# Second half's first layer norm computed in the turned layout: x loaded transposed, statistics spread over the partitions, in place of TensorE transposes

## The chip, the cores and the metric

The kernel runs on one core of one Trainium2 chip. The metric is device time in microseconds from the first to the last instruction of one execution. All arithmetic is float32; products are made of float32r operands (an upper and a lower part of each value).

## The reference

```python
y = _layernorm(x)                       # x: (2048, 1024), eps 1e-5
q, k, v = y @ wq, y @ wk, y @ wv        # 32 heads of 32, 4 segments of 512 tokens
# in each segment s: causal softmax attention inside the segment, and a read of the memory (M, z)
o = g * (phi(qs) @ M) / (phi(qs) @ z + 1e-6) + (1 - g) * softmax(qs @ ks.T * scale + mask) @ vs
M, z = M + phi(ks).T @ vs, z + sum(phi(ks))
h = x + o @ wo
out = h + gelu_tanh(_layernorm(_layernorm(h)) @ w1 + b1) @ w2 + b2     # d_ff 3584
```

The two layer norms of the last line stand for the block's own and the one ahead of it; the first line's is the one that the change touches.

## The kernel before

The 2048 tokens are worked off in two halves of 1024, each of two segments of 512. A half goes through four stages: attention, the output projection with the residual, the second layer norm, and the first MLP product (a scheme of fewer, larger block products: first a "lead", then 14 "pairs" of `Mixer.pair`). The second MLP product for all tokens comes at the end, in the second half.

Every product x @ w is made of three matmuls: upper by upper, upper by lower, lower by upper (`mm3`, lines 127 to 129 of the profile). So every activation and weight exists as an upper part (a cast to float32r) and a lower part (value minus upper part). The inputs of the attention, `yh` and `yl`, lie turned: 128 features on the partitions, tokens along the free dimension, 8 chunks of features by 512 tokens for each segment.

`ln1` makes them for one segment of 512 tokens. It loads four row tiles `xt` of 128 tokens by 1024 features. For each, VectorE takes mean and variance (lines 134 and 138), GpSimd makes the scale and the offset (lines 141, 142, 147), ScalarE scales the whole tile (line 182), and `ln_transpose` turns it: eight TensorE transposes in two groups of four (line 161), each group into one PSUM bank of tags "av" and "pt", then ScalarE's copy to `yh` (line 163) and VectorE's subtraction to `yl` (line 165).

The attention of a half is 16 units of 24 steps. A step is one chunk of one projection (three matmuls), and behind it whatever a table of steps (`at`, `close`) puts there: weight loads and splits (`wload`, `wsplit`, lines 688, 695, 699), score matmuls (line 569), their reduction on VectorE (571), exponentials on ScalarE (573), and so on. The steps 0 to 7 of a unit make `kps`, 8 to 15 `qps`, 16 to 23 `vps`. Units 0 and 1 read segment 0; unit 2 is the first that reads segment 1. A weight block is loaded (`wr`, two buffers), its upper part cast on VectorE or ScalarE, and its lower part made by GpSimd in four pieces of two chunks each, 128x256.

Segment 0 of the second half is normalised in the last nine pairs of the first half's MLP; segment 1 is begun there and goes on in units 0 and 1 of the second half's attention. There `interleave` and a counter take one piece of the side work per so many steps of the main work: 0.17 per step (three matmuls) in the pairs, 0.55 per step in the attention. The order of instructions on each engine is the order in which the program emits them (`in_order`), and each engine waits in that order.

In the pairs, each `Mixer.pair` makes five products of 12 matmuls (line 1014) in 20 steps: `dps` in a bank of tag "pt" (two banks), `bps` in tag "d" (three). VectorE adds out of these banks (lines 1038, 1156, 1169), ScalarE applies the activation (1031), GpSimd combines weights (1126 to 1129), ScalarE and VectorE split them (1141, 1142).

Of the kernel before, what the change touches and what calls it, by code (L numbers as in the profile page):

```python
# [4 lines left out]

# [12 lines left out]
P = 128  # L18
S = 2048
D = 1024  # L20
# [27 lines left out]
def raw(ap):  # L48
    return ap.bitcast(F32)


def build(tc, x, wq, wk, wv, wo, beta, w1, b1, w2, b2, out):
    nc = tc.nc
    top = ExitStack()
    const = top.enter_context(tc.tile_pool(name="const", bufs=1))
# [100 lines left out]
    def ln_transpose(src, xh, xl, t4, tags, slow=False):  # L156
        for c in range(2):
            pt = ln_bank(tags).rearrange("p (a b) -> p a b", a=4)
            for i in range(4):
                k = 4 * c + i  # L160
                nc.tensor.transpose(pt[:, i, :], src[:, k * P:(k + 1) * P], ident)
            hi = xh[:, 4 * c:4 * c + 4, t4 * P:(t4 + 1) * P]
            nc.scalar.copy(hi, pt)
            yield
            nc.vector.tensor_tensor(xl[:, 4 * c:4 * c + 4, t4 * P:(t4 + 1) * P], pt, raw(hi),  # L165
                                    op=ALU.subtract)
            if slow:
                yield
# [36 lines left out]
    def chain(*gens):  # L205
        for g in gens:
            yield from g
# [6 lines left out]
    def ln1(half, sl, delay=0, aside=None, gap=1):  # L214
        xs = []
        for t in range(4):
            xt = lnp.tile([P, D], F32, tag="ln", name="xt", bufs=4)
            r0 = half * HT + (4 * sl + t) * P
            nc.sync.dma_start(xt, x[0, r0:r0 + P, :])
            xs.append(xt)  # L220
        for _ in range(delay):
            yield

        def home():
            if ("y", half, sl) not in acts:
                acts["y", half, sl] = acts["y", sl] = seg_tiles(sl, "y")
            return acts["y", sl]

        yield from ln_tiles(lnp, xs, None, None, False, act=True, aside=aside, gap=gap,
                            fold=lambda src, t4: ln_transpose(src, *home(), t4, ("av", "pt", "pt"), slow=True))  # L230

    def opening():

# [1203 lines left out]
    for half in range(2):  # L1437
# [15 lines left out]
        if half == 0:  # L1453
            nc.sync.dma_start(mz_dram, acts["mz"])
        ab.release()
        zx = acts["zx"] = tc.alloc_tile_pool(name=f"zx{half}", bufs=1, side="right", reuse_waits="tile")
        mq = tc.alloc_tile_pool(name=f"mq{half}", bufs=1, side="right", reuse_waits="tile")
        pp = tc.alloc_tile_pool(name=f"post{half}", bufs=1, reuse_waits="tile")
# [93 lines left out]
    top.close()  # L1552


_INS = ["A_x", "A_wq", "A_wk", "A_wv", "A_wo", "A_beta", "B_w1", "B_b1", "B_w2", "B_b2"]


# [16 lines left out]
```

## Time and profile before

| what | value |
|---|---|
| three runs | 2185.11, 2191.39, 2191.93 us; median 2191.39 |
| the profiled execution | 2187.23 us, span 2185.5 us |
| TensorE busy | 2157.7 us, 99% of the span |
| VectorE, ScalarE, GpSimd busy | 1349.0, 1102.1 and 959.7 us |
| moved by DMA | 376.20 MB, mean 172 GB/s |

A busy TensorE is one with a matmul in flight: matmuls overlap, so a duration of 0.39 us belongs to a matmul that starts 0.227 us after the one before it. In rows of the chain, the times are those by which the chain went on. In this profile the engines are PE (TensorE), DVE (VectorE), ACT (ScalarE), POOL (GpSimd) and SP (the queue that issues most DMAs); L161 is line 161 of the kernel. A pointed bracket names what ended the idle time before an instruction.

### The profile page before, as it was taken

The page shows a single profiled execution, that of the slowest core. Times are in us where ns is not written, and L with a number is a line of the kernel's source. Part 1 is how long each engine was busy: PE and PEld are TensorE (multiplying, and loading weights), DVE is VectorE, ACT ScalarE, POOL GpSimd, SP SyncE. Part 2 cuts the span into 40 slices and gives each one's busy share as a digit, 9 for nine tenths or more (in the row PEclk, how much of TensorE's full clock was granted, in tenths as well). Part 3 has the DMA queues.
Part 4 walks back from the last instruction along what each step waited for, and adds up shares of the span by engine and source line. Part 5 has one row for each costly group of instructions (what it writes and reads, how often), then busy time and mean ns, then how long its engine had stood idle before and what let it go on. Part 6 is the DMA issues. An engine that isn't in the chain of part 4 may idle for free.

```text
span 2185.5 us, 33210 instructions
## 1 busy us (share of the span) xinstructions
PE 2157.7 (99%) x10937; PEld 1750.4 (80%) x10937; DVE 1349.0 (62%) x2696; ACT 1102.1 (50%) x2433; POOL 959.7 (44%) x1206
## 2 busy tenths in 40 slices
PE   7999999999999999999999999999999999999999
PEld 6777777778888888877777768888887888888887
DVE  6766666665745556766667655745666665576653
ACT  5777777762543445777777752643443232322221
POOL 5534345562444434533335561534446544256330
PEclk9999999999999999999999999999999999999999
DMA  6544445664465655544444663575569865676762
GB/s 182 134 106 107 105 107 136 190 203 164 154 207 155 187 158 147 136 107 109 106 108 133 198 197 141 173 217 162 171 199 373 274 226 185 190 244 230 250 222 92
DMA packets 352405, 376.20 MB, mean 172 GB/s; under 512 B 27214, under 2 KB 244330, under 8 KB 352234
## 3 DMA queue, kind: packets, MB, share of 16 engines
q1 hardware_dynamic: 288778, 336.98, 50.7%
q10 hardware_dynamic: 63456, 37.10, 5.6%
q8 instruction: 87, 1.43, 0.3%
q14 instruction: 84, 0.69, 0.1%
HBM read 241.27 MB, written 82.38 MB: 148 GB/s over the span
## 4 chain that ended last, share of the span: by engine, by line
PE 91%; DVE 2%; DMA 2%; POOL 2%; ACT 1%; issue 1%; SPq 0%; ACTq 0%; DVEq 0%; POOLq 0%
PE po L1410 22%; PE bps L1014 10%; PE cps L1014 7%; PE dps L1014 7%; PE pst L619 4%; PE po L633 3%; PE pqk L569 3%; PE kps L127 3%; PE vps L127 3%; PE qps L127 3%; PE kps L128 3%; PE pwo L127 2%; PE kps L129 2%; PE vps L128 2%; PE pwo L129 2%; PE pwo L128 2%
## 5 line engine op out<-in xcount | busy, mean ns | idle before, releaser
L571 DVE CUSTOM_DVE_ANT_0 pqk<-pqk,mask 128x512 f32<-128x512 f32 (+2 forms) x384 | 216.9, 565 | 241.6 <-PE pqk L569 214.8
L573 ACT ACTIVATE junk<-pqk,mx 128x512 f32<-128x512 f32 (+2 forms) x384 | 225.2, 587 | 134.7 <-DVE mx L571 128.2
L626 POOL TENSOR_SCALAR_AFFINE_SELECT e<-e 128x128 f32<-128x128 f32 (+1 forms) x384 | 137.6, 359 | 268.9 <-ACT e L622 254.1
L699 POOL TENSOR_TENSOR wl<-wr,wh 128x256 fp32r<-128x256 f32 x268 | 202.1, 770 | 108.7 <-PE pqk L569 85.8
L622 ACT ACTIVATE e<-pst 128x384 f32<-128x384 f32 (+1 forms) x384 | 200.8, 529 | 70.9 <-PE pst L619 69.5
L1420 DVE TENSOR_TENSOR c<-c,po 128x512 f32<-128x512 f32 x160 | 105.4, 684 | 156.7 <-PE po L1410 153.9
L569 PE MATMUL pqk<-ks,qs 96*128 96x512 f32 (+2 forms) x384 | 138.6, 361 | 5.7 <-ACT junk L573 3.0
L619 PE MATMUL pst<-qs,ks 104*128 104x512 f32 (+3 forms) x512 | 140.9, 318 | 1.0 <-ACT e L622 0.4
L619 PEld LDWEIGHTS pst<-qs,ks 104*128 104x128 f32 x512 | 95.7, 188 | 34.7 <-ACT e L622 10.7
L1410 PE MATMUL po<-w2h,zh 128*128 128x512 f32 x378 | 120.9, 389 | 0.4 <-DVE zh L1350 0.4
L1267 POOL TENSOR_TENSOR w2r<-w2r 128x512 f32<-128x512 f32 x54 | 84.6, 1579 | 72.3 <-DMA w2r<-in_B_w 72.3
L127 PE MATMUL kps<-yh,wh 128*128 128x512 f32 (+1 forms) x264 | 113.5, 430 | 0.0
L127 PE MATMUL qps<-yh,wh 128*128 128x512 f32 x256 | 113.2, 442 | 0.0
L1014 PE MATMUL bps<-zh,sb 128*128 128x512 f32 x336 | 110.9, 391 | 0.0
L1014 PE MATMUL bps<-zh,sa 128*128 128x512 f32 x336 | 110.8, 390 | 0.0
L1126 POOL TENSOR_TENSOR s<-r 128x512 f32<-128x512 f32 x28 | 44.3, 1583 | 141.0 <-DVE sa L1142 81.3
L127 PE MATMUL vps<-yh,wh 128*128 128x512 f32 x256 | 105.0, 410 | 0.0
L1410 PE MATMUL po<-w2h,hl 128*128 128x512 f32 x322 | 103.2, 390 | 0.7 <-DVE hl L1350 0.4
L128 PE MATMUL kps<-yl,wh 128*128 128x512 f32 (+1 forms) x264 | 102.8, 389 | 0.5 <-DVE yl L165 0.4
L129 PE MATMUL kps<-yh,wl 128*128 128x512 f32 (+1 forms) x264 | 102.2, 387 | 0.0
L128 PE MATMUL qps<-yl,wh 128*128 128x512 f32 x256 | 101.0, 394 | 0.0
L128 PE MATMUL vps<-yl,wh 128*128 128x512 f32 x256 | 100.8, 394 | 0.0
(271 smaller groups left out, 6204.0 us busy)
## 6 DMA issues: line engine op xcount, KB each, us to landing
hr<-h_dram SPq DMA_DIRECT2D x112, 448.0 KB, 5.5
w2r<-in_B_w SPq DMA_DIRECT2D x122, 256.0 KB, 4.2
r<-in_B_w SPq DMA_DIRECT2D x56, 512.0 KB, 4.6
ks<-kk SPq DMA_DIRECT2D x360, 64.0 KB, 2.0
qs<-qq SPq DMA_DIRECT2D x360, 64.0 KB, 2.0
h_dram<-ht ACTq DMA_DIRECT2D x84, 256.0 KB, 3.6
wx<-in_B_w SPq DMA_DIRECT2D x56, 256.0 KB, 3.5
o_dram<-side SPq DMA_DIRECT2D x52, 256.0 KB, 4.2
```

The costliest lines, as they stand in the source:

```text
L127: nc.tensor.matmul(ps, ah, bh, start=first, stop=False)
L128: nc.tensor.matmul(ps, ah, bl, start=False, stop=False)
L129: acts["mm"] = nc.tensor.matmul(ps, al, bh, start=False, stop=last)
L569: nc.tensor.matmul(ps, u["qs"][0:96, j, i * P:(i + 1) * P], u["ks"][0:96, j, 0:n], start=True, stop=True)
L571: nc.vector.tensor_tensor_reduce(out=ps, in0=ps, in1=mask[:, 512 - n:512], op0=ALU.add, op1=ALU.min, scale=-SCALE, scalar=3.0e38, accum_out=m)
L573: at(now[0] + 1, lambda: nc.scalar.activation(acts["junk"][:, :n], ps, AF.Exp, bias=m, scale=-1.0, accum_out=u["mx"][:, 1, i, j:j + 1]))
L619: nc.tensor.matmul(ps[:, o:o + 512 - P * jk], u["ks"][:, j, jk * P:(jk + 1) * P], u["qs"][:, j, jk * P:512], start=True, stop=True)
L622: nc.scalar.activation(e, ps[:, :w], AF.Exp, scale=SCALE)
L626: nc.gpsimd.affine_select(d, d, pattern=[[0, 2], [1, P]] if n == 2 else [[1, P]], compare_op=ALU.is_ge, fill=0.0, base=0, channel_multipli ...
L699: nc.gpsimd.tensor_tensor(l[:, c], wr[:, c], raw(h)[:, c], op=ALU.subtract)
L1014: nc.tensor.matmul(ps, x_[:, c, :], y_[:, c, :], start=first and c == 0 and n == 0, stop=last and c == 3 and n == 2, skip_group_check=True)
L1410: nc.tensor.matmul(ps, x_[:, k], y_[k], start=opens and k == 0 and i == 0, stop=closes and k == self.KP - 1 and i == 2, skip_group_check=True)
```

## The change

The host passes a second copy of x, transposed (`xt_`). The new class `Columns` normalises a segment without turning its tiles. From the row tiles it takes only the statistics: `rn` holds, for each of 4 tiles, the scale r of 128 tokens and the offset -mean * r (8 columns). One TensorE transpose turns `rn` to 8x128, ScalarE copies it out, a DMA stores it to DRAM, and another loads it back to all partitions as `rows`: 512 scales and 512 offsets. The turned x is loaded in four tiles `xc` of 128 partitions by two chunks by 512 tokens, and for each, `apply` multiplies by the scales and adds the offsets, `upper` copies to `yh`, `lower` subtracts to `yl`.

A table of steps says when each piece is emitted. Both segments' statistics, loads and `rows`, and the four rounds of segment 0, come in the last nine pairs, one step per 1/0.22 steps of the pairs; there VectorE multiplies and adds. The four rounds of segment 1 come in the attention, where VectorE multiplies and GpSimd adds; with 0.55 pieces per step they reach to about step 38.

```diff
+    rn_dram = {k: dram.tile([8, P], F32, name=f"rn_dram{k[0]}{k[1]}") for k in ((1, 0), (1, 1))}
...
+    class Columns:
+        def __init__(self, half, sl):
+            self.half, self.sl, self.plan = half, sl, {}
+            self.rn = acts["rnp"].tile([P, 8], F32, name="rn", bufs=2)
...
+        def load(self, t):
+            self.xs[t] = lnp.tile([P, D], F32, tag="ln", name="xt", bufs=4)
+            r0 = self.half * HT + (4 * self.sl + t) * P
+            nc.sync.dma_start(self.xs[t], x[0, r0:r0 + P, :])
+        def stats(self, t):
...
+            nc.vector.bn_aggr(mv, st)
...
+            nc.gpsimd.tensor_tensor(r, v[:, 0:1], mhalf, op=ALU.pow)
+            nc.gpsimd.tensor_scalar(rn[:, 4 + t:5 + t], mv[:, 0:1], -1.0, r, op0=ALU.mult, op1=ALU.mult)
+        def turn(self):
+            ps = psum.tile([P, 512], F32, tag="av", name="prn", bufs=1)[0:8, 0:P]
+            nc.tensor.transpose(ps, self.rn, ident)
+            self.rt = acts["rnp"].tile([P, P], F32, name="rt", bufs=1)[0:8, :]
+            nc.scalar.copy(self.rt, ps)
+        def keep(self):
+            nc.sync.dma_start(rn_dram[self.half, self.sl], self.rt)
+        def spread(self):
+            self.rows = acts["rnp"].tile([P, 2, 512], F32, name="rows", bufs=1)
+            nc.sync.dma_start(self.rows.rearrange("p a n -> p (a n)"),
+                              rn_dram[self.half, self.sl].rearrange("k p -> (k p)").partition_broadcast(P))
+        def columns(self, c):
+            t0 = self.half * HT + 512 * self.sl
+            self.ws[c] = w = lnp.tile([P, 2, 512], F32, tag="ln", name="xc", bufs=4)
+            nc.sync.dma_start(w, xt_[256 * c:256 * c + 256, t0:t0 + 512].rearrange("(c p) n -> p c n", p=P))
+        def apply(self, c, i, eng):
+            w, row = self.ws[c], self.rows[:, i, :].unsqueeze(1).to_broadcast([P, 2, 512])
+            eng.tensor_tensor(w, w, row, op=ALU.add if i else ALU.mult)
...
+        def upper(self, c):
+            nc.scalar.copy(self.home(0, c), self.ws[c])
+        def lower(self, c):
+            nc.vector.tensor_tensor(self.home(1, c), self.ws[c], raw(self.home(0, c)), op=ALU.subtract)
...
+        def columns_at(self, *steps, lag, add):
+            for c, m in enumerate(steps):
+                self.at(m, partial(self.apply, c, 0, nc.vector))
+                self.at(m + 1, partial(self.apply, c, 1, add))
+                self.at(m + lag, partial(self.upper, c))
+                self.at(m + lag + 1, partial(self.lower, c))
...
-            acts["ahead"] = ln1(1, 1, gap=2)
-            interleave(chain(*(mixer.pair(j) for j in range(HP - 9, HP))),
-                       chain(ln1(1, 0, 2), islice(acts["ahead"], 3)), 0.17)
+            acts["rnp"] = tc.alloc_tile_pool(name="rn1", bufs=1, reuse_waits="tile")
+            one, two = Columns(1, 0), Columns(1, 1)
+            for t in range(4):
+                one.at(0, partial(one.load, t))
+                one.at(6 + t, partial(one.columns, t))
+                two.at(19 + 3 * t, partial(two.load, t))
+                two.at(25 + 3 * t, partial(two.columns, t))
+            one.rows_at(3, 4, 5, 6, turn=9, keep=10, spread=12)
+            one.columns_at(15, 18, 21, 24, lag=2, add=nc.vector)
+            two.rows_at(22, 25, 28, 31, turn=34, keep=35, spread=37)
+            interleave(chain(*(mixer.pair(j) for j in range(HP - 9, HP))), steps(one, two), 0.22)
+            two.columns_at(4, 8, 12, 16, lag=3, add=nc.gpsimd)
+            acts["ahead"] = steps(two)
...
+    inputs = {**inputs, "A_xT": np.asarray(inputs["A_x"])[0].T}
```

Two places in the order of instructions, first as it stands before, then with the change. GpSimd, from the last split of the first weight blocks into unit 1 of the second half's attention (`wl` are the low parts of weight blocks; `v`, `nb` belong to the layer norm, `xc` are the turned columns, `mask` and `pat` constants):

```order
L104 TENSOR_TENSOR wl<-wr,wh 128x1024 x2
L141 TENSOR_SCALAR v<-mv 128x1
L142 TENSOR_TENSOR v<-v,mhalf 128x1
L147 TENSOR_SCALAR nb<-mv,v 128x1
L341 MEMSET mask 128x512
L518 MEMSET pat 8x4
L342 AFFINE_SELECT mask<-mask 128x128
L519 AFFINE_SELECT pat<-pat 8x4
L521 AFFINE_SELECT pat<-pat 8x4
L699 TENSOR_TENSOR wl<-wr,wh 128x256 x4
L141 TENSOR_SCALAR v<-mv 128x1
L142 TENSOR_TENSOR v<-v,mhalf 128x1
```

```order
L104 TENSOR_TENSOR wl<-wr,wh 128x1024 x2
L428 MEMSET mask 128x512
L605 MEMSET pat 8x4
L429 AFFINE_SELECT mask<-mask 128x128
L606 AFFINE_SELECT pat<-pat 8x4
L608 AFFINE_SELECT pat<-pat 8x4
L786 TENSOR_TENSOR wl<-wr,wh 128x256 x4
L281 TENSOR_TENSOR xc<-xc,rows 128x1024 x2
L786 TENSOR_TENSOR wl<-wr,wh 128x256 x5
L281 TENSOR_TENSOR xc<-xc,rows 128x1024
L786 TENSOR_TENSOR wl<-wr,wh 128x256 x4
L281 TENSOR_TENSOR xc<-xc,rows 128x1024
```

Where small pieces of the layer norm stood, four additions of 128x1024 stand: two of them between the value weights of unit 0 (the first four pieces) and the key weights of unit 1 (the first four of the next five). VectorE, from unit 0's first lower part (`side<-kps`) to the first score reduction (`pqk`):

```order
L440 TENSOR_TENSOR side<-kps,side 128x512
L682 CAST ks_8733<-pat 8x2048
L165 TENSOR_TENSOR yl_8801<-pt,yh_8800 128x4x128
L382 SCALAR_TENSOR_TENSOR pk,zc<-e,r 128x512
L165 TENSOR_TENSOR yl_8801<-pt,yh_8800 128x4x128
L682 CAST ks_8734<-pat 8x2048
L134 BN_STATS st<-xt 128x6 x2
L138 BN_AGGR mv<-st 128x2
L440 TENSOR_TENSOR side<-qps,side 128x512
L682 CAST identr<-ident 128x128
L695 CAST wh<-wr 128x1024
```

```order
L527 TENSOR_TENSOR side<-kps,side 128x512
L769 CAST ks_8747<-pat 8x2048
L281 TENSOR_TENSOR xc<-xc,rows 128x1024
L469 SCALAR_TENSOR_TENSOR pk,zc<-e,r 128x512
L769 CAST ks_8748<-pat 8x2048
L527 TENSOR_TENSOR side<-qps,side 128x512
L292 TENSOR_TENSOR yl_8849<-xc,yh_8848 128x1024
L281 TENSOR_TENSOR xc<-xc,rows 128x1024
L769 CAST identr<-ident 128x128
L782 CAST wh<-wr 128x1024
```

The subtractions out of PSUM and the statistics are gone; the first round's subtraction (`yl`) and the second round's multiplication (`xc`) stand ahead of the cast of unit 1's key weights (`wh`). On ScalarE the upper copy of the first round stands ahead of the copy of `qps`, and that of the second behind the two exponentials of `qps`.

## Rows read from the trace of the kernel before

**Rows 1.** The page: busy time by engine, and the chain's shares by engine.

```profile
PE 2157.7 (99%) x10937; PEld 1750.4 (80%) x10937; DVE 1349.0 (62%) x2696; ACT 1102.1 (50%) x2433; POOL 959.7 (44%) x1206
...
PE 91%; DVE 2%; DMA 2%; POOL 2%; ACT 1%; issue 1%; SPq 0%; ACTq 0%; DVEq 0%; POOLq 0%
```

**Rows 2.** Stretches: us, busy time (instructions) of each engine, clock, DMA share, GB/s.

```profile
717.00:836.60 119.60, 118.72 (x539) 97.95 (x538) 69.19 (x105) 50.60 (x77) 46.65 (x45) 1.00 0.53 156
836.60:881.60 45.00, 44.09 (x226) 36.04 (x226) 33.58 (x80) 27.19 (x61) 24.49 (x42) 1.00 0.61 162
881.60:926.60 45.00, 45.00 (x258) 36.63 (x257) 30.90 (x98) 32.20 (x91) 23.33 (x44) 1.00 0.49 129
```

**Rows 3.** Chain of waits in the pairs: start, us on the chain, engine, tile, line.

```profile
740.69 0.44 PE pt L161 x4
...
784.79 5.44 PE bps L1014 x24
...
810.77 0.70 DVE ht L1038
811.61 2.96 PE dps L1014 x12
```

**Rows 4.** The transposes of line 161 on TensorE between 700 and 900 us.

```profile
L161 PE MATMUL pt<-ident,xt x64: 270/272/273, 740.5 to 878.4; 128*128 128x128 f32 x64
```

**Rows 5.** Groups of the whole trace, by shape: busy us, mean ns | idle before.

```profile
L926 DVE TENSOR_TENSOR hb<-ht,b2c 128x1024 f32<-128x1024 f32 x16 | 19.2, 1209 | 0.5 <-DMA h_dram<-hb 0.4
...
L1126 POOL TENSOR_TENSOR s<-r 128x512 f32<-128x512 f32 x28 | 44.3, 1583 | 141.0 <-DVE sa L1142 81.3 <-DVE sb L1142 39.7 <-DMA r<-in_B_w 12.6
...
L104 POOL TENSOR_TENSOR wl<-wr,wh 128x1024 fp32r<-128x1024 f32 x2 | 4.8, 2406 | 6.5 <-issue 6.2 <-ACT wh L103 0.4
...
L695 ACT CAST wh<-wr 128x1024 fp32r<-128x1024 f32 x1 | 1.0, 1032 | 0.0
```

**Rows 6.** Timeline of VectorE in a pair: start, us, instruction.

```profile
701.11 2.99 DVE L1142 TENSOR_TENSOR sb<-s,sb 128x512 fp32r<-128x512 f32 x3 [1.85 <-ACT sb L1141]
...
707.34 0.68 DVE L1142 TENSOR_TENSOR sb<-r,sb 128x512 fp32r<-128x512 f32 x1
```

**Rows 7.** Timeline of GpSimd in the same pair.

```profile
701.93 1.61 POOL L1126 TENSOR_TENSOR s<-r 128x512 f32<-128x512 f32 x1 [5.47 <-DVE sb L1142]
```

**Rows 8.** Timeline of ScalarE in unit 0 of the second half's attention.

```profile
840.37 1.25 ACT L182 ACTIVATE xt<-xt,nb,v 128x1024 f32<-128x1024 f32 x1 [2.00 <-POOL nb L147]
...
843.86 0.59 ACT L434 CAST side<-kps 128x512 fp32r<-128x512 f32 x1
...
848.70 0.59 ACT L434 CAST side<-qps 128x512 fp32r<-128x512 f32 x1 [1.92 <-PE qps L129]
```

**Rows 9.** Timeline of VectorE in units 0 and 1.

```profile
844.48 0.69 DVE L440 TENSOR_TENSOR side<-kps,side 128x512 fp32r<-128x512 f32 x1 [5.44 <-ACT side L434]
845.21 1.40 DVE L682 CAST ks<-pat 8x2048 fp32r<-8x2048 f32 x1
...
852.53 0.69 DVE L695 CAST wh<-wr 128x1024 fp32r<-128x1024 f32 x1 [0.52 <-DMA wr<-in_A_wk]
...
858.08 0.69 DVE L695 CAST wh<-wr 128x1024 fp32r<-128x1024 f32 x1
...
868.19 0.69 DVE L695 CAST wh<-wr 128x1024 fp32r<-128x1024 f32 x1 [0.52 <-DMA wr<-in_A_wk]
```

**Rows 10.** Timeline of GpSimd: low parts of unit 1's key weights, four pieces.

```profile
853.36 3.28 POOL L699 TENSOR_TENSOR wl<-wr,wh 128x256 fp32r<-128x256 f32 x4 [0.74 <-DVE wh L695]
```

**Rows 11.** Timeline of TensorE in unit 1.

```profile
856.01 0.40 PE L129 MATMUL kps<-yh,wl 128*128 128x512 f32 x1
...
867.30 0.50 PE L569 MATMUL pqk<-ks,qs 96*128 96x512 f32 x1
...
870.47 0.44 PE L569 MATMUL pqk<-ks,qs 96*128 96x384 f32 x1 [0.83 <-ACT junk L573]
```

**Rows 12.** Timeline of the SP queue: the load of unit 2's key weights.

```profile
863.93 0.37 SPq L688 DMA_DIRECT2D wr<-in_A_wk  x1
```

More of the change, by code (lines that the diff above doesn't have):

```diff
@@ L3 @@
 from functools import partial
-from itertools import islice
 import concourse.bass as bass
@@ L49, in raw, with build @@
     return ap.bitcast(F32)
-def build(tc, x, wq, wk, wv, wo, beta, w1, b1, w2, b2, out):
+def build(tc, x, xt_, wq, wk, wv, wo, beta, w1, b1, w2, b2, out):
     nc = tc.nc
@@ L230, in ln1, with at, home, rows_at @@
                             fold=lambda src, t4: ln_transpose(src, *home(), t4, ("av", "pt", "pt"), slow=True))
+    class Columns:
+        def __init__(self, half, sl):
+            self.half, self.sl, self.plan = half, sl, {}
+            self.rn = acts["rnp"].tile([P, 8], F32, name="rn", bufs=2)
+            self.xs, self.ws = {}, {}
+        def at(self, step, *fns):
+            self.plan.setdefault(step, []).extend(fns)
+        def load(self, t):
[3 more added lines that the diff above has]
+        def stats(self, t):
+            rn = self.rn
+            st = lnp.tile([P, 2, 6], F32, name="st", bufs=3)
+            for i in range(2):
+                nc.vector.bn_stats(st[:, i, :], self.xs[t][:, 512 * i:512 * i + 512])
+            mv = lnp.tile([P, 2], F32, name="mv", bufs=3)
+            nc.vector.bn_aggr(mv, st)
+            v = lnp.tile([P, 2], F32, name="v", bufs=3)
+            r = rn[:, t:t + 1]
+            nc.gpsimd.tensor_scalar(v[:, 0:1], mv[:, 1:2], 1.0, EPS, op0=ALU.mult, op1=ALU.add)
+            nc.gpsimd.tensor_tensor(r, v[:, 0:1], mhalf, op=ALU.pow)
[18 more added lines that the diff above has]
+            eng.tensor_tensor(w, w, row, op=ALU.add if i else ALU.mult)
+        def home(self, i, c):
+            if ("y", self.half, self.sl) not in acts:
+                acts["y", self.half, self.sl] = acts["y", self.sl] = seg_tiles(self.sl, "y")
+            return acts["y", self.sl][i][:, 2 * c:2 * c + 2, :]
+        def upper(self, c):
+            nc.scalar.copy(self.home(0, c), self.ws[c])
+        def lower(self, c):
+            nc.vector.tensor_tensor(self.home(1, c), self.ws[c], raw(self.home(0, c)), op=ALU.subtract)
+        def rows_at(self, *steps, turn, keep, spread):
+            for t, m in enumerate(steps):
+                self.at(m, partial(self.stats, t))
+            self.at(turn, self.turn)
+            self.at(keep, self.keep)
+            self.at(spread, self.spread)
+        def columns_at(self, *steps, lag, add):
[4 more added lines that the diff above has]
+                self.at(m + lag + 1, partial(self.lower, c))
@@ L232, in opening, with steps @@
+    def steps(*plans):
+        plan = {}
+        for p_ in plans:
+            for m, fns in p_.plan.items():
+                plan.setdefault(m, []).extend(fns)
+            p_.plan = {}
+        for m in range(max(plan) + 1):
+            for f in plan.get(m, ()):
+                f()
+            yield
     def opening():
@@ L1455, in build @@
         ab.release()
+        if "rnp" in acts:
+            acts.pop("rnp").release()
         zx = acts["zx"] = tc.alloc_tile_pool(name=f"zx{half}", bufs=1, side="right", reuse_waits="tile")
@@ L1552, in build @@
     top.close()
-_INS = ["A_x", "A_wq", "A_wk", "A_wv", "A_wo", "A_beta", "B_w1", "B_b1", "B_w2", "B_b2"]
+_INS = ["A_x", "A_xT", "A_wq", "A_wk", "A_wv", "A_wo", "A_beta", "B_w1", "B_b1", "B_w2", "B_b2"]
 def kernel(**inputs):
```

## The prediction

> **What bounds the kernel now.** I read the page's busy times and its chain first. TensorE is busy for 99% of the span and carries 91% of the chain that ends last [rows 1]: an instruction taken off TensorE is worth its own time, and anything that makes TensorE wait costs in full. Then the stretches around the change: the last nine pairs of the first half, the 45 us of the first two attention units of the second half, and the 45 us behind them [rows 2]. TensorE idles about 0.9 us in each of the first two and nothing in the third, so no later idle time absorbs a loss. The chain and the timelines, read next, show which wait ends last.
>
> In the pairs the 24 matmuls of a piece take 5.44 us, 0.227 us each, back to back [rows 3]. Two things interrupt them: groups of four transposes, 0.44 us of chain each, and one wait of 0.84 us (811.61 - 810.77) for VectorE's addition out of `dps`, which holds the "pt" bank that the next `dps` needs; the transposes take banks from the same tag.
>
> In the attention, TensorE waits once, at 870.47, for 0.83 us [rows 11]. The chain behind it: the load of a weight block is issued at 863.93 [rows 12], VectorE casts it at 868.19 [rows 9], and the score reduction queued behind that cast lets TensorE go on. That load starts when GpSimd has finished the low parts of an earlier block (two buffers). So this place is tight on VectorE, ScalarE and GpSimd, though none is the busiest.
>
> **The change, part by part.** *Transposes.* 64 leave TensorE between 740 and 878 us [rows 4], 16 groups, half in the pairs, half in the attention: 8 x 0.44 = 3.5 us in each. Two transposes of the 128x8 statistics come in; they are not in the trace. Bounds: nothing, or a whole group (0.44) each; I take 0.1 each, a quarter of a group.
>
> *Banks.* The layer norm's transposes no longer take "pt" banks in the pairs, so the 0.84 us wait goes, with the pipeline refill behind it about 0.9.
>
> *Pairs, the other engines.* VectorE gets eight 128x1024 multiplications and additions and four subtractions at 1.21 us, the row of the same shape with all operands in SBUF [rows 5], for eight 512-wide subtractions: some 9 us more over about 40 us in which it is busy 58% [rows 2]. Two in a row delay an addition out of PSUM by 2.4 us; it has the 2.72 us of the next product. I cost this at nothing; if that cover fails the price is the excess over 2.72, some 0.4 us (2.4 + 0.69 - 2.72), at four places, 1.6 us. SP gets eight column loads and two row loads (5 MB) and two stores of 4 KB; the DMA engines are half busy here [rows 2]. The store waits for ScalarE and the row load for the store, with weight loads queued behind; they are issued a pair ahead, so this costs nothing unless they slip by most of a pair (13.6 us).
> Pairs: -3.5 - 0.9 + 0.2 = -4.2 us.
>
> *Attention.* Off VectorE go three tiles' statistics and eight subtractions, off ScalarE the scaling of row tiles. On come four rounds: VectorE multiplies, GpSimd adds, ScalarE copies the upper part, VectorE subtracts. Each round crosses three in-order queues, and the next multiplication stands behind the last subtraction. GpSimd's addition is 128x1024. The nearest rows are 2.41 us (the same shape, alone) and twice 1.58 (half the shape, beside VectorE) [rows 5]: bounds 2.41 and 3.17. I take 2.8, their middle, since VectorE is busy three quarters of this stretch.
>
> First with 2.41, in time of the trace before. ScalarE loses the 1.24 us scaling at 840.37, so its copy of `kps` comes 1.0 us earlier, near 842.9, and VectorE's subtraction at 843.5 instead of 844.48 [rows 8, 9]. Then the 1.40 us cast [rows 9], the multiplication (846.7), the addition (849.1), the upper copy at 1.03 [rows 5] (850.2). Behind that copy ScalarE has the copy of `qps`: it ends at 850.8 where it ended at 849.3 [rows 8]. VectorE: its subtraction, the first round's subtraction, the second multiplication: 853.8. Second addition: 856.2. Only then GpSimd makes the low parts of unit 1's key weights: four pieces took 3.28 us from 853.36 [rows 10], now the first is there at 857.0. TensorE, without four groups and their refills, wants it at 854.2 (24 steps of 0.68 from 836.7, 0.7 for the small matmuls, and two matmuls), so it waits 2.8 us. Before, the matmul ran at 856.01 [rows 11]: it is now 1.0 late. **A new wait takes the place of the transposes.**
>
> It grows. Second upper copy 857.3, subtraction 858.7, multiplication 859.9; the query weights' cast, behind both on VectorE, ends at 861.1 (858.8 before [rows 9]). Its first low piece 861.9, third addition 864.3, upper copy 865.3, subtraction and multiplication 867.8; then a reduction, a cast and the key subtraction: 869.5. ScalarE's two pieces after it: 870.7, when TensorE's 512-wide score matmul can start; before, 867.30 [rows 11]. The weight load of [rows 12] is issued at 866.6, when the query pieces end, its cast ends at 872.2, reduction and exponential follow, and the score matmul of 870.47 starts at 873.7: 3.2 late. Three groups behind it are gone, -1.3: the attention loses 1.9. With 2.8 per addition, three on the path: 1.9 + 3 x 0.39 = 3.1 us. The fourth falls behind this point and I cost it at nothing: the values are first read in unit 2, some 8 us later.
>
> *Sum:* -4.2 + 3.1 = -1.1 us, on a profiled execution of 2187.23 us that lies 4.2 below the median of the three runs, 2191.39. I forecast against the median: 2190.3, **no change**. A measurement of this kernel tells about 0.3% (6.6 us) from none.
>
> **A rule weighed.** The trace shows VectorE and GpSimd in each other's way: three 512-wide subtractions with both inputs in SBUF take 2.99 us at 701.11 where one takes 0.68, while GpSimd's additions run, the first of them for 1.61 us [rows 6, 7]. In the changed attention, by these rows, whichever of the two has started makes the other wait out its instruction. An addition of 2.41 us would then hold back the cast of unit 1's key weights (to 856.2; cast, `pq` and the first low piece then take turns, and the piece is there at 858.4 instead of 857.0), and the next subtraction and multiplication lose about a piece (0.75) each: some 2.9 us more on the path. [...] By the rule the sum would be -4.2 + 3.1 + 2.9 = +1.8, 2193.2; by the rows without it -1.1. Since the trace shows it only where both queues are full, I leave it to a rival.
>
> **The rivals.**
> *The rounds are hidden.* If TensorE never waits for the rounds, the attention gains 3.5 and the 0.9 us of idle time: -4.2 - 4.4 = -8.6, 2182.8. For it: VectorE's total work there hardly changes (about 10 us off, 10 on), and the rounds have 36 steps. Against it: the order puts the second addition ahead of the key weights' low parts, and that piece is wanted at 854.2. It decides whether the second addition ends by 853.4.
> *GpSimd's additions and VectorE lock each other out.* The end on the other side. Price +2.9 as above, and +2.3 if the additions take 3.17 on top of 2.41 (instead of the 1.2 counted, so +1.1 more), and up to 0.75 for each of the other two subtractions: +2.9 to +5.5 over the forecast, 2193.2 to 2195.8, slower than before. For it: rows 6 and 7. Against it: most VectorE work in the attention has one operand in PSUM. It decides from the point where the score matmul of 870.47 comes over 5.5 us late: less the 1.3 of the three groups, that uses up the pairs' 4.2.
> *The pairs give nothing.* Column loads held up on SP, or VectorE's bursts, cost TensorE what the transposes gave (4.2): 2194.5. Against it: the loads are a step behind their buffers' release.
>
> **How the numbers follow.** Forecast 0.50; hidden 0.25; locked out 0.20; no gain in the pairs 0.05. Over 0.3% faster needs -6.6: nearly all of the hidden case and a little of the forecast's lower edge, 0.22. Over 0.3% slower needs +6.6: only the upper ends of the last two cases with the scatter of the median (the runs before span 6.8 us), 0.10. Within: 0.68. The range reaches down to the hidden case, 2182, and up past the locked one, 2197; the forecast's own range, with additions of 2.41 to 3.17 and 1.6 for the bursts, is 2189 to 2193.
>
> **What would show it.** Right: 16 groups of transposes gone, the pairs' stretch some 4 us shorter without the wait for `dps`, and TensorE waiting 2 to 4 us at the first key matmuls of unit 1 for GpSimd, and at the score matmuls of unit 1 for ScalarE. Wrong: the two units shorter by 3 us or more (the additions start earlier than I have them or take less than 2.4), or additions near 4 us (locked out). Waits in the pairs for `sa`, `sb` or `bps` would break the first term.

## The result, and the profile after

The changed kernel takes 2196.64 us (median of six runs, 2195.48 to 2199.91); the kernel before takes 2187.28 (six runs, the three of the table above among them). The ratio is 1.0043, 95% interval [1.0027, 1.0058]: slower by 9.4 us. Forecast were 1.1 us less, called no change, with 6.6 us as the least that counts as a change. That the range holds the time is luck: it was laid around 2191.39, 4.1 us above the median of the six runs. As a difference to the kernel before it reached from -9.4 to +5.6 us.

The page of the changed kernel, busy time by engine and the chain by engine, answers to [rows 1]: TensorE lost 1.4 us of work and 1% of the span, VectorE gained 31 us, and VectorE's share of the chain went from 2 to 3%.

```profile
PE 2156.3 (98%) x10875; PEld 1746.6 (80%) x10875; DVE 1380.2 (63%) x2700; ACT 1091.7 (50%) x2419; POOL 967.0 (44%) x1210
...
PE 89%; DVE 3%; DMA 3%; issue 2%; ACT 2%; POOL 1%; SPq 0%; ACTq 0%; DVEq 0%; POOLq 0%
```

The stretches that answer to [rows 2]. The first, cut at 717 as before, ends 4.9 us later, the second is 52.1 us long instead of 45.0, and in the third, 45 us as before, TensorE is busy throughout. In the last four lines, cut out of the first two stretches, the column behind GpSimd's, TensorE's granted clock, is 0.53 to 0.55 of full speed (half clock below): there a 128x512 matmul starts 0.43 us after the one before it, against 0.227 at 1.00. In [rows 2] it is 1.00 everywhere.

```profile
717.00:841.50 124.50, 117.26 (x498) 94.71 (x497) 83.96 (x115) 44.45 (x70) 50.03 (x52) 0.97 0.64 185
841.50:893.60 52.10, 45.05 (x194) 35.73 (x193) 40.35 (x71) 23.74 (x54) 34.18 (x37) 0.90 0.51 138
...
893.60:938.60 45.00, 45.00 (x258) 36.64 (x257) 30.77 (x98) 32.37 (x92) 23.94 (x44) 1.00 0.50 131
...
776.00:779.60 3.60, 3.60 (x10) 2.82 (x9) 2.76 (x5) 2.49 (x4) 0.67 (x1) 0.53 0.57 154
793.00:796.80 3.80, 3.80 (x12) 2.92 (x11) 1.60 (x2) 2.79 (x4) 3.70 (x3) 0.55 0.58 197
861.00:868.30 7.30, 5.54 (x15) 4.57 (x16) 7.30 (x12) 2.49 (x5) 5.00 (x6) 0.53 0.59 145
878.40:882.00 3.60, 3.60 (x12) 2.66 (x12) 2.49 (x4) 2.03 (x8) 3.60 (x4) 0.53 0.36 81
```

TensorE's waits in the changed kernel, us in total, times, longest (`u` is VectorE's addition out of a `bps` bank, `sa` and `sb` are sums of weights, of which ScalarE casts the upper and VectorE makes the lower part): all 14 pairs,

```profile
PE bps L1101 <- DVE u L1256: 5.4, 3, 2.5
PE bps L1101 <- ACT sa L1228: 1.8, 1, 1.8
```

and the two units of the attention (`junk` is ScalarE's exponential of the scores, `qs` the queries, stored and loaded back by DMA):

```profile
PE pqk L656 <- ACT junk L660: 2.2, 1, 2.2
PE kps L129 <- POOL wl L786: 2.0, 1, 2.0
PE pqk L656 <- DMA qs<-side: 1.3, 1, 1.3
PE pqk L656 <- DMA qs<-qq: 1.3, 1, 1.3
```

So the pairs, forecast at -4.2, lost 7.3 us: from their first matmul on `bps` (641.25 before, 638.78 after) to the first `kps` of the second half (836.66 and 841.53) they take 195.4 before and 202.8 after. The sum: idle time 7.2 instead of 0.9; two stretches at half clock, 3.6 x 0.47 + 3.8 x 0.45 = 3.4, an estimate of what full clock would have saved there; transposes -3.3; together +6.4. The rest, 0.9, is about what the refill of TensorE costs: the last matmul ahead of a wait takes its whole 0.39 us instead of 0.227, and the second behind it starts 0.33 us after the first (792.28 and 792.61), together 0.27 us for each of three waits more. The attention, forecast at +3.1, lost 7.1 (45.01 and 52.15 to the first `kps` of unit 2). Of the 14.5 us together the medians show 9.4. 2.5 are gone before the pairs begin, ahead of every changed instruction, and 3.4 come back between unit 2 and the end, where both kernels run the same code; why two profiled executions differ so there is not known.

### The profile page after: what moved, and what is told of

It is laid out like the page before. It is cut to its first block, busy times and chain, and to the rows that moved or that the text cites. A ratio compares the mean times of both kernels' runs of the same rounds, so it can differ in the third digit from the quotient of the medians.

```text
span 2194.1 us, 33104 instructions
## 1 busy us (share of the span) xinstructions
PE 2156.3 (98%) x10875; PEld 1746.6 (80%) x10875; DVE 1380.2 (63%) x2700; ACT 1091.7 (50%) x2419; POOL 967.0 (44%) x1210
## 4 chain that ended last, share of the span: by engine, by line
PE 89%; DVE 3%; DMA 3%; issue 2%; ACT 2%; POOL 1%; SPq 0%; ACTq 0%; DVEq 0%; POOLq 0%
PE po L1497 23%; PE bps L1101 9%; PE cps L1101 7%; PE dps L1101 6%; PE pst L706 3%; PE po L720 3%; PE pqk L656 3%; PE kps L127 3%; PE kps L129 3%; PE kps L128 3%; PE pwo L127 2%; PE qps L127 2%; PE pwo L129 2%; PE pwo L128 2%; PE vps L127 2%; PE qps L128 2%
## 5 line engine op out<-in xcount | busy, mean ns | idle before, releaser
L129 PE MATMUL qps<-yh,wl 128*128 128x512 f32 x256 | 101.2, 395 | 0.0
```

The lines of the kernel that those rows point to most:

```text
L129: acts["mm"] = nc.tensor.matmul(ps, al, bh, start=False, stop=last)
```

## The experiments

The stages of every run, as above (first `bps` to first `kps`, and from there to unit 2), with the medians beside those of the kernel before in the same session:

| run | pairs | attention | us | before | ratio, 95% |
|---|---|---|---|---|---|
| before | 195.4 | 45.0 | 2187.28 | | |
| changed | 202.8 | 52.2 | 2196.64 | 2187.28 | 1.0043 [1.0027, 1.0058] |
| e1_pairs_only | 201.1 | 45.3 | 2190.84 | 2186.49 | 1.0031 [1.0018, 1.0044] |
| e3_no_rounds | 193.4 | 43.0 | 2181.11 | 2186.49 | 0.9978 [0.9969, 0.9988] |
| e4_placed | 201.4 | 52.0 | 2200.28 | 2186.49 | 1.0073 [1.0056, 1.0089] |
| e5_dve_adds | 202.2 | 48.8 | 2195.58 | 2186.49 | 1.0047 [1.0032, 1.0062] |
| e6_wide_slots | 195.6 | 51.9 | 2192.23 | 2186.67 | 1.0026 [1.0017, 1.0036] |
| e7_rounds_early | 195.7 | 44.6 | 2182.98 | 2186.67 | 0.9984 [0.9974, 0.9994] |
| e8_rounds_spread | 195.7 | 44.6 | 2185.02 | 2186.67 | 0.9994 [0.9984, 1.0003] |
| e9_filled | 202.8 | 52.2 | 2199.54 | 2186.67 | 1.0064 [1.0047, 1.0081] |
| e10_thirteen | 192.7 | 43.0 | 2180.67 | 2185.68 | 0.9975 [0.9965, 0.9985] |
| e11_pool_rounds | 197.7 | 52.2 | 2194.73 | 2185.68 | 1.0042 [1.0028, 1.0056] |
| e12_rows_psum | 199.5 | 51.8 | 2196.14 | 2187.00 | 1.0046 [1.0031, 1.0061] |
| e13_thirteen_psum | 190.7 | 43.4 | 2179.54 | 2187.00 | 0.9967 [0.9955, 0.9978] |

A stage is read from one traced execution of each run. Where runs have the same code in a stage they agree: the pairs of the changed kernel took 202.2 to 202.8 us in three runs (e5 and e9 have them too), its attention 51.8 to 52.2 in five (e4, e6, e11, e12). Behind unit 2 all fourteen run the same code, and there the traces span 1300.1 to 1305.1 us; so a gain of a few us in a stage need not show in a run's time.

The theory to begin with: VectorE's long pieces of the layer norm (one multiplication, addition or subtraction of 128x1024 each) stand ahead of the MLP's own short ones in its queue, which it works off in order. The place where the longest wait of the pairs begins shows it. VectorE in the changed kernel, start, us, instruction:

```profile
769.80 2.31 DVE L292 TENSOR_TENSOR yl<-xc,yh 128x1024 fp32r<-128x1024 f32 x1
772.03 2.29 DVE L281 TENSOR_TENSOR xc<-xc,rows 128x1024 f32<-128x1024 f32 x1
774.24 0.68 DVE L1256 TENSOR_TENSOR u<-bps,p1r 128x512 f32<-128x512 f32 x1
```

GpSimd and TensorE beside it:

```profile
770.99 2.25 POOL L1215 TENSOR_TENSOR s<-r,r 128x512 f32<-128x512 f32 x1
```

```profile
774.97 0.50 PE L1101 MATMUL bps<-zh,sb 128*128 128x512 f32 x1 [2.52 <-DVE u L1256]
```

The addition `u` out of `bps` (u3 in the expectations) frees the bank into which TensorE accumulates next; it starts at 774.24, behind two pieces of 2.3 us each. Alone such a piece takes 1.22; here GpSimd's sum of weights, 1.29 where nothing overlaps it, takes 2.25 in the same time. With 1.22 each `u` would have started 2.2 us earlier, and 0.4 of the 2.52 us of waiting would be left. Ahead of the next wait (1.78 us, ended at 792.28) nothing doubles, and the queue alone is too long: three long pieces and a tile's statistics stand among the weights' low parts and ahead of `u`, which TensorE needs by 790.3. VectorE again:

```profile
784.92 1.29 DVE L1229 TENSOR_TENSOR sb<-s,sb 128x512 fp32r<-128x512 f32 x2 [1.85 <-ACT sb L1228]
786.13 1.22 DVE L292 TENSOR_TENSOR yl<-xc,yh 128x1024 fp32r<-128x1024 f32 x1
787.27 1.22 DVE L281 TENSOR_TENSOR xc<-xc,rows 128x1024 f32<-128x1024 f32 x1
788.40 0.68 DVE L1229 TENSOR_TENSOR sb<-s,sb 128x512 fp32r<-128x512 f32 x1
789.00 1.22 DVE L281 TENSOR_TENSOR xc<-xc,rows 128x1024 f32<-128x1024 f32 x1
790.14 1.28 DVE L251 BATCH_NORM_STATS2 st<-xt 128x6 f32<-128x512 f32 x2
...
791.58 0.65 DVE L1256 TENSOR_TENSOR u<-bps,p1r 128x512 f32<-128x512 f32 x1
```

So there are two candidates, the order of the pieces and their doubling beside GpSimd, and two outside rivals, the added loads and a clock that falls by itself.

**e1_pairs_only**: segment 1 as before, segment 0 as changed.

```diff
-            two.columns_at(4, 8, 12, 16, lag=3, add=nc.gpsimd)
-            acts["ahead"] = steps(two)
+            acts["ahead"] = ln1(1, 1, gap=2)
```

> First segment's layer norm in the new way in the pairs, second segment's in the old way in the attention. The changed kernel's attention begins 4.9 us later than before (841.5 against 836.7) and its two units take 7.1 us longer (52.1 against 45.0). Theory 'two separate losses' (VectorE's queue in the pairs, the four rounds in the attention): the attention begins near 841.5 again with the same kind of waits in the pairs and stretches at half clock behind them, and the two units take 45 us: about 2187.3 + 4.9 = 2192 us. Rival 'one loss' (the attention is slow because it starts behind disturbed pairs): the units take over 49 us here too, 2196 us.

The pairs lose 5.7 us and the attention 0.3: two separate losses.

**e3_no_rounds**:

```diff
-            eng.tensor_tensor(w, w, row, op=ALU.add if i else ALU.mult)
+            pass
```

> As the changed kernel, but the sixteen multiplications and additions of row statistics are left out (the layer norm of the second half is not applied); loads, statistics, stores of the rows, upper and lower parts stay. Theory 'VectorE's queue' (its 1.2 to 2.3 us pieces stand ahead of the subtractions and additions that TensorE waits for): no wait over 0.5 us in the pairs, no half-clock stretch there, the attention begins near 832.5 (what the transposes and the bank were worth, 4.2 us), the two units take about 41 us: 2187.3 - 4.2 - 4.4 = 2179 us. Rival 'loads' (5 MB more on SP's queue and the DMA engines hold up the weights): the attention still begins after 840. Rival 'clock falls by itself' (without the transposes): half-clock stretches stay though the waits are gone.

The loads, stores and statistics stay, and the pairs take 193.4: the loads are not the cause. One wait over 0.5 us is left (1.2), and no stretch at half clock, here or in the attention (granted clock 1.00 in both), so the clock doesn't fall for want of transposes. TensorE's waits in its pairs:

```profile
PE bps L1101 <- DVE u L1256: 1.5, 2, 1.2
```

In the attention the gain stops at 2.0 us of the 4.4 that eight groups of transposes and 0.9 us of idle time come to: TensorE reaches the score matmuls earlier and waits there for ScalarE (1.0) and for the loads of `qs` (1.2).

**e4_placed**: each piece at a fixed step of a pair, VectorE's behind `u`.

```diff
+                one.at(at(p, 8), partial(one.apply, c, 0, nc.vector))
+                one.at(at(p, 9), partial(one.apply, c, 1, nc.vector))
+                one.at(at(p, 13), partial(one.lower, c))
...
+            interleave(chain(*(mixer.pair(j) for j in range(HP - 9, HP))), steps(one, two), 1.0)
```

> As the changed kernel, but the pieces of the pairs stand at fixed places of a pair, VectorE's multiplication, addition and subtraction only behind the addition u3 that TensorE waits for first (never in the ten steps ahead of it). The same work and the same loads. Theory 'VectorE's queue': the waits and the half-clock stretches in the pairs go, the attention begins near 832.5 instead of 841.5, its two units still take 52: 2187.3 - 4.2 + 7.1 = 2190 us. Rival 'loads', or VectorE simply too full: the attention begins after 838, 2195 us.

A miss. The waits for `u` are gone, and others take their place. The transpose of the statistics stood too near behind the last of them (TensorE):

```profile
746.48 0.38 PE L262 MATMUL prn<-ident,rn 128*8 128x128 f32 x1 [3.35 <-POOL rn L258]
```

and the subtraction and a tile's statistics, placed late in a pair, delayed the two additions that end the pair; ScalarE's activation of their sums stands ahead of the casts of the next pair's weights, for which TensorE then waits (1.8, 1.1). The slack behind `u` is not the only one that counts.

**e5_dve_adds**:

```diff
-            two.columns_at(4, 8, 12, 16, lag=3, add=nc.gpsimd)
+            two.columns_at(4, 8, 12, 16, lag=3, add=nc.vector)
```

> As the changed kernel, but the four additions of the attention go to VectorE instead of GpSimd. Theory 'lockout': GpSimd's four additions of 2.4 to 2.9 us stand ahead of the low parts of the weights and hold VectorE's two-SBUF-input work (a copy of 1.22 took 3.32 us, a product of 0.69 took 2.87); with 1.21 us each on VectorE the round is 1.2 to 1.7 us shorter, the wait for wl (2.0) goes, and the two units take 45 to 47 instead of 52: about 2191 us. Rival 'VectorE full': VectorE is busy 40.4 of 52.1 us, its score reductions come later still behind two pieces in a row, the units take 51 or more: 2196 us or over.

Between the two: 48.8 us, 3.3 less than with GpSimd's additions. The wait for `wl` falls from 2.0 to 0.4; the waits for ScalarE's score pieces, which follow VectorE's reductions, rise from 2.2 to 4.2. The granted clock is 1.00 in these two units, so the 3.3 us can't be put down to the doubling alone. In time the run shows nothing that could be told from the changed kernel.

**e6_wide_slots**: twelve pairs, one piece at a time where VectorE was idle. **e7_rounds_early** and **e8_rounds_spread**: besides, segment 1 is multiplied and added in the last three pairs; only upper copies and subtractions stay in the attention.

```diff
+                one.at(at(p, 9), partial(one.apply, c, 0, nc.vector))
+                one.at(at(p, 17), partial(one.apply, c, 1, nc.vector))
+                one.at(at(p + 1, 4), partial(one.upper, c))
+                one.at(at(p + 1, 8), partial(one.lower, c))
...
+                two.at(at(p, y), partial(two.apply, k // 2, k % 2, nc.vector))
+            for c in range(4):
+                two.at(1 + c, partial(two.upper, c))
+                two.at(2 + c, partial(two.lower, c))
```

> As the changed kernel, but the pieces of the pairs are spread over twelve pairs instead of nine, one VectorE piece at a time at the places of a pair where the earlier traces show VectorE idle (behind u3, behind the additions that end a pair, ahead of the third low part), upper copies behind the third cast on ScalarE, and the transposes of the statistics two thirds of a pair behind the last statistics (in the run with fixed places TensorE waited 3.3 us for them). Theory 'VectorE's and ScalarE's queues': no wait over 0.5 us in the pairs, no half-clock stretch there, first product of the pairs to the attention in 192 us (202.8 in the changed kernel, 195.4 before), the attention as in the changed kernel, 52 us: 2187 - 3.5 + 7.1 = about 2190.5 us. Rival 'VectorE too full' or 'loads': over 198 us for the pairs, 2195 us or more.

> The same pairs, and the second segment's four multiplications and additions moved into the last three pairs, both on VectorE; the attention has only the four upper copies and four subtractions left, in its first steps. Theory 'rounds cost the attention': no wait for wl, two units in 43 us or less (45.0 before, 43.0 in the run without rounds): with the pairs at 192 about 2187 - 3.5 - 2.5 = 2181 us, faster than both. Rival 'upper and lower parts are enough to hold up ScalarE and VectorE': the units take over 45, 2185 us.

> As the run before, but the four upper copies and subtractions are spread over the first 20 of the attention's steps instead of the first five. If what counts is that no piece stands ahead of a score reduction or a weight cast, this is the worse or the better of the two by where they fall: within 1 us of it by the theory 'rounds cost the attention' (the pieces are short, 1.05 and 1.21), 2 us slower by 'each piece ahead of a reduction costs its own length'.

The pairs no longer lose but don't gain 3.5 either: four waits are left in two neighbouring pairs, those that hold three pieces and a tile's statistics. TensorE's waits in e6's pairs:

```profile
PE bps L1101 <- DVE u L1256: 1.2, 2, 0.6
PE bps L1101 <- ACT sa L1228: 1.1, 1, 1.1
PE bps L1101 <- ACT sb L1228: 0.5, 1, 0.5
```

The attention without multiplications and additions takes 44.6, where the same pairs with them take 51.9 (e6): the rounds cost 7.3 us there. That is more than the theory of e7 allowed (43) and less than its rival (over 45). Early or spread makes no difference in the stage (44.58, 44.62); the medians are 2.0 us apart, with intervals that overlap.

**e9_filled**: needless matmuls in the wait for `wl`.

```diff
+                if half and n == 1 and c == 0:
+                    for _ in range(9):
+                        nc.tensor.matmul(u[name + "ps"], w[0][:, k, :], yh[:, k, :], start=True, stop=True)
```

> The changed kernel with nine needless matmuls (2.0 us) put ahead of the first key product of unit 1, that is into the wait for GpSimd's low part (2.0 us at 860.7): their sums are thrown away by the start of the product behind them. Theory 'half clock follows TensorE's wait': without the idle time the stretch at half clock behind it (861.5 to 868.3) goes or shrinks by half, some 15 matmuls by 0.2 us: the two units take 49 instead of 52, 2193.5 us. Rival 'the clock falls for another reason': the stretch stays, and the units take 52 or, if the wait was shorter on TensorE than the nine, up to 54.

The theory was right on the clock and wrong on the time. With the wait filled the clock stays up where it had fallen (861.00 to 868.30, at 0.53, in the changed kernel); the stretch behind 878 stays at half clock:

```profile
861.00:868.30 7.30, 6.09 (x29) 4.50 (x27) 7.30 (x11) 2.26 (x4) 5.17 (x5) 1.00 0.58 142
...
878.60:882.10 3.50, 3.50 (x11) 2.62 (x11) 2.55 (x5) 1.93 (x8) 3.50 (x4) 0.51 0.39 86
```

But the units take 52.2 as before, which the rival had foretold for another reason: the next score matmul, which had not waited at half clock, now does.

```profile
868.60 0.50 PE L656 MATMUL pqk<-ks,qs 96*128 96x512 f32 x1 [1.44 <-ACT junk L660]
```

So half clock in that stretch cost nothing: the chain through the other engines set the pace.

**e10_thirteen**: e7 over thirteen pairs, statistics apart from the rounds.

```diff
-            interleave(chain(*(mixer.pair(j) for j in range(HP - 12, HP))), steps(one, two), 1.0)
+            interleave(chain(*(mixer.pair(j) for j in range(HP - 13, HP))), steps(one, two), 1.0)
```

> The run with early rounds again, but over thirteen pairs, so that no pair holds three VectorE pieces and a tile's statistics. There the two pairs that held both lost 3.4 us together (four waits of 0.9 to 1.5), with pieces of 2.0 to 2.3 us where GpSimd's weight sums ran at the same time, behind the statistics on its queue; the pairs with pieces alone lost nothing. Theory 'queues, with VectorE and GpSimd doubling each other's pieces': those waits go, first product of the pairs to the attention in 192 to 193 us (195.7 there), attention 44.6 as there: 2180 us, faster than both kernels. Rival 'any three pieces in a pair cost': the waits stay and the time is 2183 again.

As expected but for two waits of 0.6 us that are left: pairs 192.7, and faster than both kernels. (The 0.9 to 1.5 of the expectation run from the start of the matmul ahead of a wait, 0.39 us more than the idle time shown above.) It is the place that counts here, for the doubling went on: nine of this run's twenty pieces in the pairs took 1.8 us or more, against three of twelve in the changed kernel. Durations in ns, lowest, median and highest:

```profile
L281 DVE TENSOR_TENSOR xc<-xc,rows x16: 1212/1217/2240, 704.3 to 829.8; 128x1024 f32<-128x1024 f32 x16
L292 DVE TENSOR_TENSOR yl<-xc,yh x4: 2141/2242/2244, 717.9 to 761.3; 128x1024 fp32r<-128x1024 f32 x4
```

The attention is e7's program and took 43.0 this time: 0.7 us of waiting for `qs` instead of 1.5, and 1.1 for ScalarE instead of 2.0.

**e11_pool_rounds**:

```diff
-            one.columns_at(15, 18, 21, 24, lag=2, add=nc.vector)
+            one.columns_at(15, 18, 21, 24, lag=4, add=nc.gpsimd, mult=nc.gpsimd)
```

> The changed kernel with the multiplications and additions of the pairs on GpSimd instead of VectorE, two steps more for each round; the attention is unchanged. GpSimd is busy 50 of 124 us there and gets some 20 more. Theory 'pieces ahead of u3 on VectorE's queue': with eight pieces off that queue at least the waits of 2.5 and 2.0 us behind them go, the pairs take 198 us or less (202.8 in the changed kernel): 2192 us. Rival 'each blocks the other, whoever holds the piece': VectorE's low parts and subtractions, with two SBUF inputs, wait out GpSimd's 2.4 us instructions, the pairs take 202 us or more: 2197 us or more.

The pairs take 5.0 us less than with the pieces on VectorE, as the theory had it; in the run's time none of it shows. And as the rival had it, VectorE's low parts now wait for GpSimd's long pieces. Two that take 0.69 each alone:

```profile
769.86 4.61 DVE L1229 TENSOR_TENSOR sa<-s,sa 128x512 fp32r<-128x512 f32 x2
```

**e12_rows_psum**: the changed kernel with segment 0's rows in PSUM. **e13_thirteen_psum**: e10 with both segments' rows there.

```diff
+        def lift(self):
+            self.prow = [psum.tile([P, 512], F32, tag="qk", name="prow", bufs=2) for _ in range(2)]
+            for i in range(2):
+                nc.scalar.copy(self.prow[i], self.rows[:, i, :])
```

> The changed kernel, but before the rounds of the pairs ScalarE copies segment 0's rows into two PSUM banks that are idle there, so that VectorE's eight multiplications and additions have one SBUF input instead of two; order, steps and engines stay. Theory 'doubling beside GpSimd': of the twelve long pieces in the pairs three multiplications or additions took 1.7 to 2.3 us instead of 1.2; they go back to 1.2 to 1.3, the waits behind them (2.5 and 1.8 us) shrink by about 1 each, one stretch at half clock goes: pairs 199 to 200 us (202.8 in the changed kernel), 2193.5 us. Rival 'order alone': the pieces were slow for another reason or it does not matter, pairs within 0.5 of 202.8.

> The run over thirteen pairs, with both segments' rows in PSUM in the same way. There two waits of 0.6 us for u3 are left, and VectorE pieces beside GpSimd's sums took up to 2.2 us. Theory 'doubling': the two waits go, the pairs take 191.5 instead of 192.7, the attention 43 to 44.6 as before: 2179.5 us. Rival: ScalarE's four extra copies and the load of the rows that they wait for hold up the casts: 193.5 or more, 2181.5 us.

e12 leaves order and engines alone. The multiplication that took 2.29 takes 1.21, though GpSimd runs beside it; the subtraction ahead of it, still with two SBUF inputs, doubles as before. VectorE, and GpSimd in the same time:

```profile
771.79 2.31 DVE L298 TENSOR_TENSOR yl<-xc,yh 128x1024 fp32r<-128x1024 f32 x1
774.02 1.21 DVE L287 TENSOR_TENSOR xc<-xc,prow 128x1024 f32<-128x1024 f32 x1
775.15 0.68 DVE L1262 TENSOR_TENSOR u<-bps,p1r 128x512 f32<-128x512 f32 x1
```

```profile
772.97 2.25 POOL L1221 TENSOR_TENSOR s<-r,r 128x512 f32<-128x512 f32 x1
```

The wait behind it falls from 2.52 to 1.65:

```profile
775.88 0.50 PE L1107 MATMUL bps<-zh,sb 128*128 128x512 f32 x1 [1.65 <-DVE u L1262]
```

The next, behind which nothing had doubled, stays (1.76), the third grows (2.35 instead of 1.80), the fourth goes. The pairs take 199.5. They had lost 11.5 us against the forecast (7.3 and the 4.2 that the transposes should have given): 3.3 of these are the doubling of additions and multiplications, with one stretch at half clock (the granted clock is 0.99 from 717.0 to 838.7, where the changed kernel has 0.97 from 717.0 to 841.5), and 8.2 are order, with the one subtraction that doubles. The time shows nothing of the 3.3, which is what its interval spans. In e13 no wait is left: TensorE is busy in all of the 190.00 us shown, nearly the whole of its pairs, and the sixteen pieces take 1203 to 1221 ns, where those of the changed kernel on VectorE took 1210 to 2299.

```profile
640.00:830.00 190.00, 190.00 (x840) 157.10 (x839) 138.65 (x181) 73.81 (x119) 85.13 (x76) 1.00 0.67 195
```

```profile
L287 DVE TENSOR_TENSOR xc<-xc,prow x16: 1203/1210/1221, 706.3 to 829.8; 128x1024 f32<-128x1024 f32 x16
```

Its median is 7.5 us under that of the kernel before, the largest gain of all; e10's 5.0 is within its interval. In the pairs placing the pieces over thirteen pairs gave 10.1 us (202.8 to 192.7), and then the rows in PSUM 2.0.

## Why the prediction was wrong

The stages lost 14.5 us where the forecast gained 1.1: the pairs are off by 11.5, the attention by 4.0. The prediction's own signs came: TensorE waited 2.0 us for GpSimd at the first key matmuls of unit 1 and 2.25 for ScalarE at its score matmuls, and waits for `bps` and `sa` stood in the pairs, which it had named as breaking its first term.

**Transposes and bank in the pairs, -4.2: right.** With nothing in the way (e13) the pairs take 4.7 us less.

**The step that failed: "I cost this at nothing", with the 2.72 us of the next product as cover for VectorE's bursts.** In its place stand 6.3 us more of idle TensorE, and an estimated 3.4 us of half clock behind it. Three things were missed. The 2.4 us of two pieces in a row was a price without GpSimd; GpSimd's sums run in these pairs, and the very rows cited against the attention, [rows 6, 7], were from a pair. The cover was counted from the moment an addition is ready, as if VectorE's queue were empty then: up to three pieces stood there with the low parts of weights. And it was counted for `u` alone: an addition that ends a pair is followed by ScalarE's activation and then the casts that the next pair needs (e4, which has no wait for `u`, shows this one). The fail price, the excess of one burst at four places (1.6), took no such queue into account, and the chance of 0.05 that the pairs gain nothing was far too small.

**Column loads, rows and SP's queue at nothing: right** (e3).

**Attention, +3.1: right in kind, too small in size; the rival in which the two engines lock each other out was nearer.** In time of the trace before (4.87 us earlier), the second addition ended at 856.7 (forecast with 2.41: 856.2), and TensorE waited for `wl` until 857.9, for 2.0 us instead of 2.8, being 1.3 late already through `qs`. From there the steps fall behind: the query weights' cast ended at 863.1 instead of 861.1, the key subtraction at 872.1 instead of 869.5, and the score matmul that was wanted at 870.7 (871.9 with additions of 2.8) started at 873.3 (878.14):

```profile
878.14 0.50 PE L656 MATMUL pqk<-ks,qs 96*128 96x512 f32 x1 [2.25 <-ACT junk L660]
```

2.0 of these 2.6 us are there by the query weights' cast, and they came from here. VectorE, then GpSimd:

```profile
851.80 3.32 DVE L769 CAST ks<-pat 8x2048 fp32r<-8x2048 f32 x1
855.64 0.69 DVE L527 TENSOR_TENSOR side<-qps,side 128x512 fp32r<-128x512 f32 x1 [0.51 <-ACT side L521]
...
858.65 0.69 DVE L782 CAST wh<-wr 128x1024 fp32r<-128x1024 f32 x1
859.25 2.87 DVE L469 SCALAR_TENSOR_TENSOR pq<-e,r 128x512 f32<-128x512 f32 x1
```

```profile
851.25 2.79 POOL L281 TENSOR_TENSOR xc<-xc,rows 128x1024 f32<-128x1024 f32 x1 [2.88 <-DVE xc L281]
858.67 2.90 POOL L281 TENSOR_TENSOR xc<-xc,rows 128x1024 f32<-128x1024 f32 x1 [4.63 <-DVE xc L281]
```

The cast `ks` and the product `pq` each wait out the addition. Only `pq` stood on the path: it put 2.2 us into VectorE's queue, which had no gap from there to the query weights' cast. Behind `ks` VectorE still waited 0.51 us for ScalarE. With the additions on VectorE (e5) they take 1.22 and 0.69:

```profile
852.81 1.22 DVE L769 CAST ks<-pat 8x2048 fp32r<-8x2048 f32 x1
...
858.81 0.69 DVE L469 SCALAR_TENSOR_TENSOR pq<-e,r 128x512 f32<-128x512 f32 x1
```

That rival gave the attention +6.0 to +8.6; it lost 7.1. Part of that is luck: the instruction that it saw held up, the key weights' cast, took its 0.69 us (858.65), the additions took 2.36 to 2.90 and not the nearly 4 that would have shown it, and no run takes the doubling alone out of the attention. A multiplication with its rows in PSUM took 1.21 us beside GpSimd's 2.25 in e12, and sixteen took 1203 to 1221 ns in e13; the cast `ks`, whose one input is in SBUF, took 3.32 beside 2.79. What spoke against that rival in the prediction, that most VectorE work of the attention has an operand in PSUM, was beside the point: one of the few instructions that have none stood on the path.

**The hidden rival, 2182.8: not with this order, and its price was too high.** Without rounds on the path the attention gained 0.4 to 2.0 us (e3, e7, e10, e13), not 4.4: in these runs TensorE waits 2.0 to 3.6 us for the loads of `qs` and for scores, where it waited 0.9 before.

Still open: how the attention's 4.0 us beyond the forecast divide between the doubling and the order, and the 5 us by which equal code differs between profiled executions.

## What to carry to other kernels

Work that is moved onto an engine with idle time is paid by what stands behind it in that engine's queue: list, for one period, what each piece delays and who waits for that, and put it where that chain is slack; in one order the pairs lost 7.3 us; in another, with more pieces and more of them doubled, they gained 2.7 (e10). Where VectorE and GpSimd are active at once, price a VectorE piece with both inputs in SBUF as such a piece was measured here (2.29 us where it takes 1.22 alone, with GpSimd's sum at 2.25 instead of 1.29), or give it one input in PSUM (1.21 beside 2.25): that brought 3.3 us in the first order and 2.0 in the second. And before an instruction taken off a busy TensorE is counted as gain, look at what it covered: in the attention more than half of the gain went into the next waits.

## What was not expected of the hardware

TensorE's granted clock fell to 0.53 to 0.55 of full speed in four stretches, within the windows of 3.6 to 7.3 us shown above, where the kernel before had 1.00 [rows 2]; each began in a wait of TensorE or soon behind one (of 2.52, 1.78, 2.00 and 2.25 us, in their order), and where the wait for `wl` was filled with needless matmuls the stretch ran at 1.00 (e9). Not every wait brought it: behind the 1.80 us that ended at 806.9 the clock stayed at 1.00. In the pairs the two stretches cost 3.4 us on top of the waits by the estimate above, which no run tests alone; in the attention the one that was removed cost nothing. Behind the first two stretches the clock was back at 1.00 while matmuls ran (779.6 to 782.0 and 796.8 to 799.0).
